# Block-sparse attention with a split-weight feed-forward layer: dense visits that take half of the keys for four heads

## The chip, the cores and the metric

One core of a Trainium2 chip runs the whole program. The metric is the device time of one execution in microseconds (us), the median of several runs; lower is better. Its engines are TensorE (PE, with its weight loads shown as PEld), VectorE (DVE), ScalarE (ACT), GpSimd (POOL) and SyncE (SP, which here only issues DMAs).

## The reference

Attention over 4 batches, 8 heads, 768 positions and a head size of 64, in float32, with a mask of 24 by 24 blocks of 32 positions; then a layer norm and a two-layer feed-forward part of widths 512, 2048, 512.

```python
mask = np.abs(blk_i - blk_j) <= window                       # window = 1
mask = mask | (blk_i == 0) | (blk_j == 0) | (blk_i == n_blocks - 1) | (blk_j == n_blocks - 1)
for qb in range(n_blocks):
    for kb in sampled_blocks[qb]:                            # 3 per row
        mask[qb*block:(qb+1)*block, kb*block:(kb+1)*block] = True
scores = np.where(mask, scale * (q @ k.T), -1e9)
attn = softmax(scores)                                       # row maximum subtracted
x = (attn @ v), heads side by side
xn = (x - mu) / np.sqrt(var + 1e-06) * g_ln
out = x + np.maximum(xn @ w_ch1, 0.0) @ w_ch2
```

A row of an inner block sees at most 8 blocks of keys (256 keys). Rows of block 0 and block 23 see all 768 keys.

## The kernel before, in words

The 768 positions of a batch are reordered into six tiles of 128 rows. Five of them hold four inner blocks each; the sixth (`t == 0`) holds blocks 1, 2, 0 and 23. Tiles run in the order 1, 2, 3, 0, 4, 5 for each of the four batches. The work on a tile is cut into visits, 15 per batch and 60 in all, and a job is the visits that share one load of keys and values:

- an N job (tiles 1 to 5) has two visits, each with four heads of all 128 rows against the 256 gathered keys of each row's block;
- tile 0 has an H job (one visit: blocks 1 and 2, all eight heads, 256 gathered keys) and a D job with four dense visits (blocks 0 and 23, 64 rows, all 768 keys, two heads each, so that 2 heads x 64 rows fill 128 partitions).

Called by their place in a batch, the D visits are the first to the fourth; the N visit after them belongs to tile 4. In a visit `scores` (line 195, its matmuls in `mm`, L203) multiplies queries and keys into one two-bank PSUM tile `ps` (1024 columns), `biggest` (L233) takes the row maximum on DVE, `softmax` (L242) writes the exponentials to `p` on ACT, `turn` (L249) transposes `p` by chunks of 128 columns on PE and copies them on ACT, and, one visit later, `attn_v` (L259) multiplies with the values into `pv` and `evict` (L291) divides by the row sum on DVE (the 65th column of the values is 1).

A matmul of scores contracts over 64 partitions and has 32 output partitions: the row half of the array is the parity `j` of the head, the column group is the 32-row piece `part`. An N visit gives the two row halves in turn (`j` = 0, 1, each to its own PSUM bank). A D visit has one parity:

```python
            j = vi.r % 2
            for lo, hi in ((0, 16), (16, 24)):
                for rr in range(2):
                    pr = 2 * vi.hf + rr
                    for gg in range(2):
                        mm(j, 2 * rr + gg, 32 * lo, 32 * (hi - lo), ...)
```

The order of the work is written out by a loop over steps. In step s come the scores and the maximum of visit s, then `attn_v` and `evict` of visit s-1, then `softmax` of s, and then pieces of the feed-forward part (`ffn`: up-projection L349 into `pu`, L359 on ACT and L360 on DVE make `hh` and `hl` of it; down-projection L373 into `pd`), shared out by a fixed cost per matmul. The pieces go around `turn` of s and around the loads of the next job, which are issued in the first visit of a job (`keys`, `values`). So the keys of a D job are issued in the H visit: `keys` sends two DMAs of 12 blocks each (L134, 768 KB each) with the values (L176, 1560 KB) between them on SP's queue. There are two buffers for keys (`ks`) and for values (`vs`): the tile-5 job loads into those of the D job, in the step of the N visit after the D visits. For an N job SP sends the neighbours' keys (L144) and values (L180, L188) and twelve gathered key blocks (L153), and POOL gathers sampled value blocks with four indirect DMAs (L192) into chunks 0, 2, 4, 6 of `vs`. Every engine runs its own stream in order; the waits between engines are set by the tile framework from what each instruction reads and writes. The weights are split into two float16 parts while the first visits run.

Of the kernel before, what the change touches and what calls it, by code (L numbers as in the profile page):

```python
# [25 lines left out]
def sparse_attention_moe(  # L26
# [169 lines left out]
    def scores(vi):  # L196
# [10 lines left out]
        if vi.kind == "N":  # L207
            for pp in range(2):
                pr = 2 * vi.hf + pp
                for gg in range(4):  # L210
                    for j in range(2):
                        mm(j, gg, 512 * j + 256 * pp, 256, q[:, pr, 32 * gg : 32 * gg + 32],
                           ks[:, gg, :, 32 * pr : 32 * pr + 32])
        elif vi.kind == "H":
            for pp in range(2):
                for rr in range(2):
                    pr = 2 * pp + rr
                    for gg in range(2):
# [13 lines left out]

    def biggest(vi):  # L233
        n, w = vi.shape
        st = vi.st = sm.tile([P, 8], F32, tag="st", name=f"st{vi.i}")
        nc.vector.tensor_reduce(out=st[:, 0:n],  # L236
                                in_=vi.ps[:, 0 : n * w].rearrange("p (h k) -> p h k", k=w),
                                axis=AX.X, op=ALU.max, negate=True)
        nc.vector.tensor_scalar(out=st[:, 4 : 4 + n], in0=st[:, 0:n], scalar1=0.125,
                                scalar2=None, op0=ALU.mult)  # L240

    def softmax(vi):  # L242
        n, w = vi.shape
        for h in range(n):
            hs = slice(h * w, (h + 1) * w)
            nc.scalar.activation(p_s[:, hs], vi.ps[:, hs], AF.Exp, bias=vi.st[:, 4 + h : 5 + h],  # L246
                                 scale=0.125)

    def turn(vi):  # L249
        c = vi.shape[0] * vi.shape[1] // P  # L250
# [8 lines left out]
    def attn_v(vi):  # L259
        pt, vs = pt_s[vi.i % 2], vi.job.vs  # L260
        pv = vi.pv = ps_v.tile([P, 512], F32, tag="pv", name=f"pv{vi.i}")
        nch = 6 if vi.kind == "D" else 2
        begun = set()

        def mm(row, col, ch, vv, e, c):
# [17 lines left out]
                                mm(2 * rr + gg, 2 * pp + j, (2 * j + pp) * 2 + c,  # L283
                                   2 * gg + c, h, c)
        else:
            for c in range(6):
                for rr in range(2):
                    for gg in range(2):
                        mm(2 * rr + gg, 0, c, c, 4 * vi.hf + 2 * rr + vi.r % 2, c)

    def evict(vi):  # L291
        n = 1 if vi.kind == "D" else 4
        u = vi.pv[:, 0 : n * 65].rearrange("p (h e) -> p h e", e=65)
        rs = sm.tile([P, n, 1], F32, tag="rs", name=f"rs{vi.i}")
        nc.vector.tensor_scalar(out=rs, in0=u[:, :, D : D + 1], scalar1=1e-9, scalar2=None,  # L295
                                op0=ALU.add)
# [5 lines left out]
            return  # L302
        for rr in range(2):
            rows = slice(64 * rr, 64 * rr + 64)
            if vi.kind == "D":
                h = 4 * vi.hf + 2 * rr + vi.r % 2
                nc.vector.tensor_scalar(out=x[64:128, h * D : (h + 1) * D], in0=u[rows, 0, 0:D],
                                        scalar1=rs[rows, 0, :], scalar2=None, op0=ALU.mult)
            else:
                for pp in range(2):  # L310
                    o = x[0:64, (4 * pp + 2 * rr) * D : (4 * pp + 2 * rr + 2) * D]
                    nc.vector.tensor_mul(o.rearrange("p (j d) -> p j d", d=D),
                                         u[rows, 2 * pp : 2 * pp + 2, 0:D],
                                         rs[rows, 2 * pp : 2 * pp + 2, :].to_broadcast([64, 2, D]))

    def norm_a(t):
        st = sm.tile([P, 10], F32, tag="ln", name=f"ln{t.n}")
# [125 lines left out]
    def add(t, kind, blocks, plan):  # L443
# [3 lines left out]
        jobs.append(job)  # L447
        for hf, r, heads in plan:
            vi = SimpleNamespace(i=len(visits), kind=kind, hf=hf, r=r, b=t.b, tile=t, job=job,
                                 heads=heads, shape=(1, 768) if kind == "D" else (4, 256))  # L450
            visits.append(vi)
            job.visits.append(vi)
            t.visits.append(vi)

    for t in tiles:
        t.visits = []
        if t.t:
            add(t, "N", list(range(4 * t.t - 1, 4 * t.t + 3)),
                [(f, f, list(range(4 * f, 4 * f + 4))) for f in range(2)])
        else:  # L460
            add(t, "H", [1, 2], [(0, 0, list(range(8)))])
            add(t, "D", [0, NB - 1], [(r // 2, r, [4 * (r // 2) + r % 2, 4 * (r // 2) + r % 2 + 2])
                                      for r in range(4)])
    NV = len(visits)
    NLAST = visits[-1].i

# [158 lines left out]
```

## Time and profile before

| what | value |
|---|---|
| median of 3 runs | 812.19 us (811.87 to 813.76) |
| the profiled execution | 817.5 us, span 815.7 us |
| PE busy | 717.9 us (88% of the span) |
| DVE, ACT, POOL busy | 314.2, 278.3, 210.8 us (39%, 34%, 26%) |
| DMA, mean over the span | 162 GB/s, 132.16 MB |
| mean granted TensorE clock | 0.955 |

The profiled execution took 5.3 us longer than the median. Times in rows are microseconds from the start of the span, durations are microseconds where not marked ns. A float32 matmul has two records in the trace, so the 16 matmuls of an N visit's scores are 32 records and the 8 of a D visit are 16. In a row of the timeline, what stands in square brackets is the idle time of the engine just before, and who ended it by the trace; "issue" means that the profile shows nothing that the engine waited for.

### The profile page before, as it was taken

To read this page: it belongs to the slowest core of one execution; us is meant where nothing else is said; L and a number is where in the kernel's file an instruction comes from. 1 tells how busy PE (TensorE), PEld (TensorE's weight loads), DVE (VectorE), ACT (ScalarE), POOL (GpSimd) and SP (SyncE) were. 2 spreads that over 40 slices of the span, in tenths; PEclk is the share of its full clock that TensorE was granted. 3 is DMA by queue.
4 is the path that set the end of the run, shared out by engine and by line. 5 is a ranking of instruction groups with operands and counts; after the bars stand their busy time and mean duration, and the time that the engine had idled before them with its cause. 6 is when DMAs were issued, how large, how long until landed. Compare 5 with 4: busy or idle time off the path is not lost.

```text
span 815.7 us, 21773 instructions
## 1 busy us (share of the span) xinstructions
PE 717.9 (88%) x9344; PEld 483.8 (59%) x9344; DVE 314.2 (39%) x618; ACT 278.3 (34%) x553; POOL 210.8 (26%) x236
## 2 busy tenths in 40 slices
PE   0545565999999999999999999989999999989997
PEld 0234432675685774765774856755866846756764
DVE  2577877334242341443341432333432332342211
ACT  0356454233343341342342431343432422333200
POOL 5276547121412103023230202023321020200000
PEclk9966786799999999999999999999999999999999
DMA  8997789138938439168947367168757194261000
GB/s 332 260 322 194 279 259 248 53 89 201 259 107 223 123 103 282 32 158 224 229 97 185 99 198 207 41 161 233 215 138 185 33 277 128 70 141 40 14 27 14
DMA packets 109792, 132.16 MB, mean 162 GB/s; under 512 B 34561, under 2 KB 80897, under 8 KB 108673
## 3 DMA queue, kind: packets, MB, share of 16 engines
q1 hardware_dynamic: 96848, 83.92, 40.0%
q0 software_dynamic: 12416, 46.51, 17.7%
q8 instruction: 74, 1.21, 0.6%
q10 hardware_dynamic: 432, 0.34, 0.1%
q14 instruction: 22, 0.17, 0.1%
HBM read 118.15 MB, written 6.29 MB: 153 GB/s over the span
## 4 chain that ended last, share of the span: by engine, by line
PE 55%; issue 20%; DMA 13%; POOL 5%; SPq 4%; DVE 2%; ACT 1%; POOLq 0%
PE pu L349 24%; PE pd L373 16%; PE ps L203 7%; DMA vs<-v 6%; PE pv L266 5%; PE pt L256 4%; DMA ks<-kT 4%; SPq L153 3%; DMA q<-qT 2%; POOL w2l L413 2%; POOL vs L192 1%; DVE ot L404 1%; POOL xl L327 1%; DMA samp<-sampled 1%; POOL ks L168 0%
## 5 line engine op out<-in xcount | busy, mean ns | idle before, releaser
L246 ACT ACTIVATE p<-ps,st 128x256 f32<-128x256 f32 (+1 forms) x192 | 83.3, 510 | 273.4 <-DVE rs L295 164.8
L349 PEld LDWEIGHTS <-w1h 128*128 128x128 f16 x1664 | 152.7, 99 | 18.6 <-issue 0.3
L373 PE MATMUL pd<-w2l,hh 128*128 128x512 f16 x384 | 147.5, 384 | 8.2 <-POOL w2l L413 4.5
L373 PE MATMUL pd<-w2h,hh 128*128 128x512 f16 x384 | 147.3, 384 | 3.1 <-ACT w2h L412 3.1
L373 PE MATMUL pd<-w2h,hl 128*128 128x512 f16 x384 | 147.5, 384 | 0.0
L360 DVE SCALAR_TENSOR_TENSOR hl<-pu,hh 128x512 f16<-128x512 f32 x96 | 66.4, 692 | 181.1 <-ACT hh L359 180.2
L373 PEld LDWEIGHTS <-hh 128*128 128x128 f16 x768 | 75.4, 99 | 94.5 <-issue 13.2
L203 PE MATMUL ps<-ks,q 64*32 64x256 f32 (+1 forms) x1664 | 83.5, 420 | 47.6 <-DMA ks<-kT 26.2
L349 PE MATMUL pu<-xth,w1l 128*128 128x256 f16 (+1 forms) x832 | 120.6, 266 | 0.0
L349 PE MATMUL pu<-xth,w1h 128*128 128x256 f16 (+1 forms) x832 | 120.6, 266 | 0.0
L349 PE MATMUL pu<-xtl,w1h 128*128 128x256 f16 (+1 forms) x832 | 120.5, 265 | 0.1
L236 DVE TENSOR_REDUCE st<-ps 128x4 f32<-128x1024 f32 (+1 forms) x60 | 69.1, 1151 | 122.6 <-PE ps L203 122.6
L192 POOL DMA_INDIRECT vs<-v,rows x88 | 87.9, 998 | 99.1 <-PE pv L266 60.5
L359 ACT ACTIVATE hh<-pu 128x512 f16<-128x512 f32 x96 | 57.4, 598 | 125.0 <-PE pu L349 110.9
L256 PE MATMUL pt<-id_sb,p 128*128 128x128 f32 x448 | 67.5, 293 | 28.4 <-ACT p L246 28.4
L203 PEld LDWEIGHTS ps<-ks,q 64*32 64x32 f32 x1664 | 34.8, 110 | 85.6 <-issue 75.0
L257 ACT COPY pt<-pt 128x512 f32<-128x512 f32 x120 | 62.1, 564 | 64.7 <-PE pt L256 56.9
L349 PEld LDWEIGHTS <-w1l 128*128 128x128 f16 x832 | 78.2, 99 | 8.5
L256 PEld LDWEIGHTS pt<-id_sb,p 128*128 128x128 f32 x448 | 54.9, 149 | 40.1 <-ACT p L246 33.4
L379 DVE SCALAR_TENSOR_TENSOR ot<-pd,x 128x512 f32<-128x512 f32 x24 | 16.6, 690 | 156.5 <-PE pd L373 156.5
L266 PEld LDWEIGHTS pv<-vs,pt 128*32 128x32 f32 x3584 | 56.5, 112 | 32.9 <-issue 24.1
L266 PE MATMUL pv<-vs,pt 128*32 128x65 f32 x3584 | 67.9, 225 | 5.1 <-issue 2.9
(75 smaller groups left out, 416.4 us busy)
## 6 DMA issues: line engine op xcount, KB each, us to landing
ks<-kT SPq DMA_DIRECT2D x28, 768.0 KB
ks<-kT SPq DMA_DIRECT2D x264, 64.0 KB
vs<-v SPq DMA_DIRECT2D x20, 780.0 KB
vs<-v SPq DMA_DIRECT2D x4, 1560.0 KB
q<-qT SPq DMA_DIRECT2D x24, 256.0 KB
out<-ot POOLq DMA_DIRECT2D x24, 256.0 KB
vs<-v SPq DMA_DIRECT2D x16, 260.0 KB
w2h<-w POOLq DMA_DIRECT2D x4, 1024.0 KB
```

The source lines that it names most:

```text
L153: nc.sync.dma_start(kv[:, gg, r, :], src[:, bass.ds(reg[NR * gg + r], 1), :] .rearrange("p o e -> p (o e)"))
L192: nc.gpsimd.indirect_dma_start(out=vs[:, 2 * gg, :], out_offset=None, in_=src, in_offset=bass.IndirectOffsetOnAxis(ap=rows[:, i : i + 1], ...
L203: nc.tensor.matmul(ps[32 * part : 32 * part + 32, col : col + n], lhs[64 * row : 64 * row + 64], rhs[64 * row : 64 * row + 64], start=True ...
L236: nc.vector.tensor_reduce(out=st[:, 0:n], in_=vi.ps[:, 0 : n * w].rearrange("p (h k) -> p h k", k=w), axis=AX.X, op=ALU.max, negate=True)
L246: nc.scalar.activation(p_s[:, hs], vi.ps[:, hs], AF.Exp, bias=vi.st[:, 4 + h : 5 + h], scale=0.125)
L256: nc.tensor.transpose(pt[:, k - lo, :], p_s[:, k * P : (k + 1) * P], id_sb)
L257: nc.scalar.copy(dst[:, lo:hi, :], pt[:, 0 : hi - lo, :])
L266: nc.tensor.matmul(pv[32 * row : 32 * row + 32, 65 * col : 65 * col + 65], pt[:, ch, 32 * row : 32 * row + 32], vs[:, vv, 65 * e : 65 * e ...
L349: nc.tensor.matmul(ph[:, j * n : (j + 1) * n], w[:, ct, fs], x[:, ct, 0:n], start=m == 0, stop=m == 3 * CT - 1, skip_group_check=True)
L359: nc.scalar.activation(dh, ph, AF.Relu)
L360: nc.vector.scalar_tensor_tensor(out=dl, in0=ph, scalar=0.0, in1=dh, op0=ALU.max, op1=ALU.subtract)
L373: nc.tensor.matmul(po, x[:, f, ts], w[:, f, :], start=m == 0, stop=m == 3 * FT - 1)
```

## The change

The four D visits of a tile stay four visits, with the same loads and the same place in the order. A visit now takes 384 keys (blocks 0 to 11 or 12 to 23, by `vi.r`) for four heads (two pairs, both parities), in place of 768 keys for two heads. The first and second visit make the two halves for heads 0 to 3, the third and fourth those for heads 4 to 7. Each half has its own row maximum. The second half of a pair works out the weights of the two halves (three small DVE operations and an exponential of 4 columns), and its `evict` scales both halves by them, adds them and divides. The first half's `evict` only copies `pv` out of PSUM.

```diff
@@ scores
-            j = vi.r % 2
-            for lo, hi in ((0, 16), (16, 24)):
-                for rr in range(2):
-                    pr = 2 * vi.hf + rr
-                    for gg in range(2):
-                        mm(j, 2 * rr + gg, 32 * lo, 32 * (hi - lo),
-                           q[:, pr, 64 + 32 * gg : 96 + 32 * gg],
-                           kx[:, lo:hi, 32 * pr : 32 * pr + 32])
+            half = slice(12 * vi.r, 12 * vi.r + 12)
+            for rr in range(2):
+                pr = 2 * vi.hf + rr
+                for gg in range(2):
+                    for j in range(2):
+                        mm(j, 2 * rr + gg, 512 * j, 384, q[:, pr, 64 + 32 * gg : 96 + 32 * gg],
+                           kx[:, half, 32 * pr : 32 * pr + 32])
@@ biggest
+        if vi.kind == "D" and vi.r:
+            a, c = vi.mate.st[:, 4:6], st[:, 4:6]
+            nc.vector.tensor_tensor(out=st[:, 6:8], in0=a, in1=c, op=ALU.min)
+            nc.vector.tensor_sub(st[:, 8:10], st[:, 6:8], a)
+            nc.vector.tensor_sub(st[:, 10:12], st[:, 6:8], c)
@@ softmax
         for h in range(n):
...
+        if vi.kind == "D" and vi.r:
+            nc.scalar.activation(vi.st[:, 12:16], vi.st[:, 8:12], AF.Exp)
@@ attn_v
-            for c in range(6):
-                for rr in range(2):
-                    for gg in range(2):
-                        mm(2 * rr + gg, 0, c, c, 4 * vi.hf + 2 * rr + vi.r % 2, c)
+            for j in range(2):
+                for c in range(3):
+                    for rr in range(2):
+                        for gg in range(2):
+                            mm(2 * rr + gg, j, 3 * j + c, 3 * vi.r + c, 4 * vi.hf + 2 * rr + j, c)
@@ evict
+        if vi.kind == "D":
+            half = sm.tile([P, 2, 65], F32, tag="half", name=f"half{vi.i}")
+            if not vi.r:
+                nc.vector.tensor_copy(half, u)
+                vi.half = half
+                return
+            wt = vi.st[:, 12:16].rearrange("p (r h) -> p r h", r=2).unsqueeze(3)
+            nc.vector.tensor_mul(half, u, wt[:, 1].to_broadcast([P, 2, 65]))
+            both = vi.mate.half
+            nc.vector.tensor_mul(both, both, wt[:, 0].to_broadcast([P, 2, 65]))
+            nc.vector.tensor_add(half, half, both)
+            u = half
@@ jobs
-                                 heads=heads, shape=(1, 768) if kind == "D" else (4, 256))
+                                 heads=heads, shape=(2, 384) if kind == "D" else (4, 256))
```

No instruction changes its place against those of other visits; the number of feed-forward matmuls per step is the same. Two places show what the streams look like. The first is PE's stream at the first D visit of batch 1 (`ps_3507` before, `ps_3521` after; `pd` is the down-projection ahead of it, `pv` the H visit's product with the values; the names in brackets are the semaphores waited for, and DMAHW6 and DMAHW0 are those of the first and the second key DMA). Before:

```order
L373 MATMUL pd_3429<-w2h,hl 128x512
L373 LDWEIGHTS hh
L373 MATMUL pd_3429<-w2l,hh 128x512
L203 MATMUL ps_3507<-ks_80,q_89 32x512 [waits DMAHW6_49,DMAHW0_49,DVE_49]
L203 MATMUL ps_3507<-ks_80,q_89 32x512 x3
L203 MATMUL ps_3507<-ks_80,q_89 32x256 x4
L266 MATMUL pv_3519<-vs_83,pt_87 32x65 [waits DMASW7_49,DVE_49,Activation_49]
```

And now:

```order
L390 MATMUL pd_3443<-w2h,hl 128x512
L390 LDWEIGHTS hh
L390 MATMUL pd_3443<-w2l,hh 128x512
L203 MATMUL ps_3521<-ks_80,q_89 32x384 [waits DMAHW6_49,DVE_49]
L203 MATMUL ps_3521<-ks_80,q_89 32x384 x7
L274 MATMUL pv_3533<-vs_83,pt_87 32x65 [waits DMASW7_49,DVE_49,Activation_49]
```

The first visit's scores no longer name the second key DMA; the second visit's do. The second place is DVE's stream in the N visit after the D visits (`st_4027` before, `st_4051` after, is that visit's maximum; then comes `evict` of the fourth D visit; `hl` is the feed-forward part). Before:

```order
L236 TENSOR_REDUCE st_4027<-ps_4010 128x4 [waits PE_49]
L239 TENSOR_SCALAR st_4027<-st_4027 128x4 [waits DVE_49]
L295 TENSOR_SCALAR rs_4055<-pv_4030 128x1 [waits PE_49]
L297 RECIPROCAL rs_4055<-rs_4055 128x1 [waits DVE_49]
L307 TENSOR_SCALAR x_94<-pv_4030,rs_4055 64x64 [waits DVE_49]
L307 TENSOR_SCALAR x_94<-pv_4030,rs_4055 64x64
L360 SCALAR_TENSOR_TENSOR hl<-pu_12_3988,hh 128x512 [waits Activation_49]
```

And now:

```order
L239 TENSOR_REDUCE st_4051<-ps_4034 128x4 [waits PE_49]
L240 TENSOR_SCALAR st_4051<-st_4051 128x4 [waits DVE_49]
L310 TENSOR_TENSOR half_4079<-pv_4054,st_3927 128x130 [waits PE_49]
L312 TENSOR_TENSOR half_3958<-half_3958,st_3927 128x130
L313 TENSOR_TENSOR half_4079<-half_4079,half_3958 128x130 [waits DVE_49]
L316 TENSOR_SCALAR rs_4083<-half_4079 128x2 [waits DVE_49]
L318 RECIPROCAL rs_4083<-rs_4083 128x2 [waits DVE_49]
L329 TENSOR_TENSOR x_94<-half_4079,rs_4083 64x128 [waits DVE_49]
L329 TENSOR_TENSOR x_94<-half_4079,rs_4083 64x128
L377 SCALAR_TENSOR_TENSOR hl<-pu_12_4012,hh 128x512 [waits Activation_49]
```

Three operations of 130 columns stand ahead of the four that were there, and `hl` behind them.

## Rows read from the trace of the kernel before

**Rows 1.** The page, part 1: busy us, share of the span, instructions.

```profile
PE 717.9 (88%) x9344; PEld 483.8 (59%) x9344; DVE 314.2 (39%) x618; ACT 278.3 (34%) x553; POOL 210.8 (26%) x236
```

**Rows 2.** Busy time by stretch: stretch, length, each engine's busy us, clock, DMA share, GB/s.

```profile
311.20:351.70 40.50, 40.50 (x509) 27.86 (x508) 12.92 (x33) 10.42 (x18) 6.99 (x10) 1.00 0.45 129
```

**Rows 3.** Timeline, PE: scores of the first D visit, batches 1, 2, 3.

```profile
311.10 1.49 PE L203 MATMUL ps<-ks,q 64*32 64x512 f32 x16 [1.29 <-DVE ot L379]
...
488.42 1.49 PE L203 MATMUL ps<-ks,q 64*32 64x512 f32 x16 [0.46 <-DMA ks<-kT]
...
666.47 1.50 PE L203 MATMUL ps<-ks,q 64*32 64x512 f32 x16 [1.20 <-DMA ks<-kT]
```

**Rows 4.** Timeline, PE: scores of a D visit, of the N visit behind, of batch 0's second.

```profile
333.70 1.49 PE L203 MATMUL ps<-ks,q 64*32 64x512 f32 x16
...
351.71 1.09 PE L203 MATMUL ps<-ks,q 64*32 64x256 f32 x32
...
145.34 2.79 PE L203 MATMUL ps<-ks,q 64*32 64x512 f32 x16
```

**Rows 5.** Timeline, SP's queue: the D job's loads in batch 1.

```profile
299.05 0.57 SPq L134 DMA_DIRECT2D ks<-kT  x1
299.81 0.38 SPq L176 DMA_DIRECT2D vs<-v  x1
300.24 0.53 SPq L134 DMA_DIRECT2D ks<-kT  x1
```

**Rows 6.** Timeline, third D visit of batch 1 on DVE, ACT and PEld.

```profile
335.26 0.96 DVE L236 TENSOR_REDUCE st<-ps 128x1 f32<-128x768 f32 x1 [0.90 <-PE ps L203]
...
336.52 0.90 ACT L246 ACTIVATE p<-ps,st 128x768 f32<-128x768 f32 x1 [2.89 <-DVE rs L295]
...
337.92 0.69 PEld L256 LDWEIGHTS pt<-id_sb,p 128*128 128x128 f32 x6
...
338.64 0.69 DVE L360 SCALAR_TENSOR_TENSOR hl<-pu,hh 128x512 f16<-128x512 f32 x1 [1.35 <-ACT hh L359]
```

**Rows 7.** Lines, by form, whole span: count, busy us, mean ns, idle before.

```profile
L246 ACT ACTIVATE p<-ps,st 128x256 f32<-128x256 f32 x176 | 68.9, 474 | 198.2 <-DVE rs L295 98.6 <-DVE st L239 73.2 <-PE pd L373 22.6
...
L312 DVE TENSOR_TENSOR x<-pv,rs 64x128 f32<-64x128 f32 x16 | 3.9, 283 | 0.2
```

**Rows 8.** Timeline, the N visit after the D visits, batch 1.

```profile
352.74 0.89 PE L266 MATMUL pv<-vs,pt 128*32 128x65 f32 x48
...
353.36 0.98 POOL L192 DMA_INDIRECT vs<-v,rows  x1 [7.90 <-PE pv L266]
...
356.90 0.34 SPq L180 DMA_DIRECT2D vs<-v  x1
356.90 0.16 DVE L295 TENSOR_SCALAR rs<-pv 128x1 f32<-128x1 f32 x1 [2.56 <-PE pu L349]
...
357.15 0.95 POOL L192 DMA_INDIRECT vs<-v,rows  x1 [0.30 <-issue]
...
359.06 0.38 PE L373 MATMUL pd<-w2l,hh 128*128 128x512 f16 x1 [0.96 <-issue]
```

**Rows 9.** Timeline, PE: the same stop in batches 0, 2 and 3.

```profile
182.56 0.38 PE L373 MATMUL pd<-w2l,hh 128*128 128x512 f16 x1 [0.97 <-issue]
...
536.35 0.38 PE L373 MATMUL pd<-w2l,hh 128*128 128x512 f16 x1 [0.91 <-issue]
...
714.42 0.38 PE L373 MATMUL pd<-w2l,hh 128*128 128x512 f16 x1 [0.73 <-issue]
```

**Rows 10.** Timeline, PE: scores of tile 5's first visit, batches 0 to 3.

```profile
196.45 1.43 PE L203 MATMUL ps<-ks,q 64*32 64x256 f32 x32 [1.19 <-issue]
...
372.90 1.52 PE L203 MATMUL ps<-ks,q 64*32 64x256 f32 x32 [1.14 <-DMA q<-qT]
...
551.10 1.52 PE L203 MATMUL ps<-ks,q 64*32 64x256 f32 x32 [2.04 <-DMA q<-qT]
...
728.56 1.52 PE L203 MATMUL ps<-ks,q 64*32 64x256 f32 x32 [1.87 <-issue]
```

More of the change, by code (lines that the diff above doesn't have):

```diff
@@ L223, in scores, with seen @@
         else:
-            j = vi.r % 2
-            for lo, hi in ((0, 16), (16, 24)):
-                for rr in range(2):
-                    pr = 2 * vi.hf + rr
-                    for gg in range(2):
-                        mm(j, 2 * rr + gg, 32 * lo, 32 * (hi - lo),
-                           q[:, pr, 64 + 32 * gg : 96 + 32 * gg],
-                           kx[:, lo:hi, 32 * pr : 32 * pr + 32])
-    def biggest(vi):
[L234 to L238, printed above, removed]
+            half = slice(12 * vi.r, 12 * vi.r + 12)
[5 more added lines that the diff above has]
+                           kx[:, half, 32 * pr : 32 * pr + 32])
+    def seen(vi):
+        n, w = vi.shape
+        return vi.ps.rearrange("p (h k) -> p h k", h=n)[:, :, 0:w]
+    def biggest(vi):
+        n = vi.shape[0]
+        st = vi.st = sm.tile([P, 16], F32, tag="st", name=f"st{vi.i}")
+        nc.vector.tensor_reduce(out=st[:, 0:n], in_=seen(vi), axis=AX.X, op=ALU.max, negate=True)
         nc.vector.tensor_scalar(out=st[:, 4 : 4 + n], in0=st[:, 0:n], scalar1=0.125,
                                 scalar2=None, op0=ALU.mult)
+        if vi.kind == "D" and vi.r:
[3 more added lines that the diff above has]
+            nc.vector.tensor_sub(st[:, 10:12], st[:, 6:8], c)
     def softmax(vi):
@@ L244, in softmax @@
         for h in range(n):
-            hs = slice(h * w, (h + 1) * w)
-            nc.scalar.activation(p_s[:, hs], vi.ps[:, hs], AF.Exp, bias=vi.st[:, 4 + h : 5 + h],
-                                 scale=0.125)
+            nc.scalar.activation(p_s[:, h * w : (h + 1) * w], seen(vi)[:, h, :], AF.Exp,
+                                 bias=vi.st[:, 4 + h : 5 + h], scale=0.125)
+        if vi.kind == "D" and vi.r:
+            nc.scalar.activation(vi.st[:, 12:16], vi.st[:, 8:12], AF.Exp)
     def turn(vi):
@@ L261, in attn_v @@
         pv = vi.pv = ps_v.tile([P, 512], F32, tag="pv", name=f"pv{vi.i}")
-        nch = 6 if vi.kind == "D" else 2
+        nch = 3 if vi.kind == "D" else 2
         begun = set()
@@ L285, in attn_v @@
         else:
-            for c in range(6):
-                for rr in range(2):
-                    for gg in range(2):
-                        mm(2 * rr + gg, 0, c, c, 4 * vi.hf + 2 * rr + vi.r % 2, c)
+            for j in range(2):
[3 more added lines that the diff above has]
+                            mm(2 * rr + gg, j, 3 * j + c, 3 * vi.r + c, 4 * vi.hf + 2 * rr + j, c)
     def evict(vi):
-        n = 1 if vi.kind == "D" else 4
+        n = 2 if vi.kind == "D" else 4
         u = vi.pv[:, 0 : n * 65].rearrange("p (h e) -> p h e", e=65)
+        if vi.kind == "D":
[10 more added lines that the diff above has]
+            u = half
         rs = sm.tile([P, n, 1], F32, tag="rs", name=f"rs{vi.i}")
@@ L304, in evict @@
             rows = slice(64 * rr, 64 * rr + 64)
[L305 to L314, printed above, removed]
+            for pp in range(n // 2):
+                h = 4 * (vi.hf if vi.kind == "D" else pp) + 2 * rr
+                o = x[64:128, h * D : (h + 2) * D] if vi.kind == "D" else x[0:64, h * D : (h + 2) * D]
+                nc.vector.tensor_mul(o.rearrange("p (j d) -> p j d", d=D),
+                                     u[rows, 2 * pp : 2 * pp + 2, 0:D],
+                                     rs[rows, 2 * pp : 2 * pp + 2, :].to_broadcast([64, 2, D]))
     def norm_a(t):
@@ L461, in sparse_attention_moe @@
             add(t, "H", [1, 2], [(0, 0, list(range(8)))])
-            add(t, "D", [0, NB - 1], [(r // 2, r, [4 * (r // 2) + r % 2, 4 * (r // 2) + r % 2 + 2])
+            add(t, "D", [0, NB - 1], [(r // 2, r % 2, list(range(4 * (r // 2), 4 * (r // 2) + 4)))
                                       for r in range(4)])
+            for r in (1, 3):
+                jobs[-1].visits[r].mate = jobs[-1].visits[r - 1]
     NV = len(visits)
```

## The prediction

> **What bounds the kernel now.** I read the page's busy shares first, then the busy time by stretch, then every idle time of PE in the timeline. The shares say PE, at 88% of the span [rows 1]. By stretch it is stricter: from the first D visit of batch 1 to the N visit behind the fourth, PE is busy 40.50 of 40.50 us at the full granted clock (1.00, the level of 2.4 GHz), DVE 12.92 and ACT 10.42 [rows 2]. A D visit there lasts 9.0 us (two of them from 333.70 to 351.71 [rows 4]), most of it feed-forward matmuls, so what PE saves inside a D visit shortens the kernel, and DVE and ACT have room. In all batches behind the start PE stands still in few places, and three kinds bear on this change: ahead of the first D visit's scores [rows 3], in the N visit behind the D visits [rows 8, 9], and ahead of tile 5's first scores [rows 10].
>
> **Scores, the main term.** A D visit's scores take 1.49 us, an N visit's 1.09 us [rows 4]. Before, a D visit uses one row half: four column groups side by side, 512 and then 256 columns, each with two records. In units of one 256-column record per group that is (2 + 1) x 2 = 6 units in a row. An N visit uses both row halves: 16 matmuls of 256 columns on eight places, 2 x 2 = 4 units. Two units less cost 0.40 us less, so a unit is 0.20 us. Now a D visit has eight matmuls of 384 columns on eight places, 1.5 x 2 = 3 units: 1.09 - 0.20 = 0.89 us, and 0.60 us saved. Twelve visits of batches 1 to 3 save 7.2 us, all on PE's path. In batch 0 the third and fourth save another 1.2 us; the second ran at the lower granted clock and took 2.79 us [rows 4], so the same share of it is 1.1 us; the first I count at nothing, since PE waits for the weight split behind it. Sum **9.5 us**. The bounds: nothing if the row halves take turns (a rival below), and 0.745 us a visit, half of 1.49, if no fixed part is left, which is 2.4 us more.
>
> **First half of the keys.** PE waits 1.29, 0.46 and 1.20 us ahead of the first D visit [rows 3]. The trace blames a key DMA in two of the three; in batch 1 it names a DVE result, and I take it for the same wait. SP sends the first key half at 299.05, the values at 299.81, the second half at 300.24 [rows 5], and the scores, which need both halves, start at 311.10 [rows 3]: 768 + 1560 + 768 KB in some 12 us. The new first visit needs the first half alone. If the DMAs land in order, it is there after a quarter of the bytes, some 3 us; if all three share the bandwidth evenly from the start, 3 x 768 of 3096 KB have moved when it lands, after 9 us, at about 308. PE comes free at 309.81 (311.10 less its wait), later than either. So the whole wait goes: **2.95 us**; the lower bound is 0. Next late would be the second half, but the second visit starts 9 us later.
>
> **Products with the values, transposes.** 24 matmuls of 65 columns and 6 transposes a visit, as before: 0.
>
> **Exponentials.** One of 768 columns took 0.90 us [rows 6], one of 256 takes 0.474 [rows 7]: 0.83 ns a column, so one of 384 takes 0.58 and two 1.16, or 0.26 more. In the third D visit of batch 1 the exponential ended at 337.42 and PE loaded weights for the transposes at 337.92 [rows 6]: 0.50 us of slack, 0.24 left. The row maximum reads as many columns (0.96). The transposes of the first head also need only the first exponential. So 0. If each of the two cost 0.90, the second would be 0.40 us late. The exponential of the weights, at most 0.47, comes behind both and holds up only copies that PE needs a visit later.
> What this row says is weighed against a rule. The Trainium skill, "TensorEngine Tiling (Array Packing)", section Performance Considerations (PSUM Bottleneck), warns that packing speeds up TensorE but not the reading of PSUM, which may become the bound. By it the 9.5 us would be partly given back as PE waits at the transposes; by the row's slack nothing is.
>
> **Combining the halves.** The first and third visits' results now need one copy in place of four operations. The second and fourth visits' need three operations more, at 0.28 us each by the 128-column row [rows 7]: 0.85 us, and three tiny ones at the maximum. In the third D visit (which evicts the second's result) DVE then idles 1.35 us ahead of `hl` [rows 6], which covers it. In the N visit `hl` follows at once, but it is for the last columns of the up-projection, and the down-projection takes three matmuls for each of 16 groups of columns in turn, and this is group 12 at the earliest, 36 matmuls on. So 0; the upper bound is 4 x 0.85 = 3.4 us if PE waits there.
>
> **The late signal.** In the N visit behind the D visits, the product with the values ends at 353.63, yet SP's values DMA and DVE's division start only at 356.90 [rows 8]. That is the end of POOL's third gather (the fourth starts at 357.15 after 0.30 us [rows 8]). PE then stands 0.96 us and goes on at 359.06, which is 0.96 us after the end of the fourth gather (357.15 + 0.95). The same stop is there in every batch, 0.97, 0.91 and 0.73 us [rows 9]. I do not know the mechanism, only that it goes with the four gathers that start while the product still runs. The change touches their start: the gathers write chunks 0, 2, 4, 6 of the D job's values, and chunks 0 and 2 belong to blocks 0 to 11, which are last read by the third D visit. So two gathers may go a visit earlier and two are left in the burst, which then ends 2.5 us sooner. I take it that PE's four stops go, **3.57 us**; the lower bound is 0.
>
> **Sum.** 9.5 + 2.95 + 3.57 = 16.0 us. The profiled execution's own time of 817.5 would become 801.5; the median stands 5.3 us below it, so the forecast is 812.19 - 16.0 = **796.2 us**.
>
> **The rivals.** A change within 0.3% (2.4 us) is what a measurement of this kernel cannot tell from none.
> - *The signal comes in time.* If SP is also released at once, the loads for tile 5 start 3.3 us earlier, and the waits of 1.19, 1.14, 2.04 and 1.87 us ahead of tile 5's scores [rows 10] go as well: 6.24 us more, **790.0 us**. For it: the loads are in SP's order behind that DMA, and all four waits are shorter than 3.3 us. Against it: two gathers remain. Chance 0.25.
> - *The stops stay.* The gathers cost PE as much in two pieces, or stops seen in a profiled execution, 5.3 us slower, are less in the timed ones: 812.19 - 12.45 = **799.7 us**. Chance 0.27.
> - *PSUM reading becomes the bound.* With 0.40 us late in 16 visits and the stops kept: 799.7 + 6.4 = **806.1 us**. The slack of 0.24 speaks against it. Chance 0.08.
> - *The row halves take turns.* Then a visit's scores keep six units, 1.49 us, and only the keys' wait goes: **809.2 us**, hardly a change. N visits with the same alternation of halves and banks speak against it. Chance 0.04.
> - *Slower: the packing breaks.* If only two of the eight matmuls ran at once, the scores would need 12 units, 1.49 + 6 x 0.20 = 2.69 us, or 1.20 us more in 16 visits: 812.19 + 19.2 - 2.95 = **828.4 us**. It decides from 1.67 us a visit on, where 16 x 0.18 eats the 2.95. Nothing in N visits speaks for it. Chance 0.03.
>
> **How the numbers follow.** The forecast has the remaining 0.33. Faster by over 0.3%: the forecast and the first three rivals, 0.93; the same 0.04; slower 0.03. The range takes in 790.0 and 799.7 with 1.5 us below and the 3.4 us bound of the combination above, 788.5 to 803.5: 0.85 of the chance.
>
> **What would show it.** Right: D visits' scores near 0.89 us; no idle ahead of the first D visit; transposes that do not wait for `p`; three operations near 0.28 us on DVE; two gathers in the fourth D visit; no stop of PE behind the D visits. Wrong: scores above 1.1 us, PE idle with ACT or DVE as releaser in D visits, or the waits of [rows 10] grown by what was saved.

## The result and the profile after

The changed kernel takes 792.12 us in the median (789.92 to 794.32), the kernel before 812.21 us beside it: a ratio of 0.9754, 95% interval 0.9727 to 0.978. That is 20.1 us less, faster by more than the 16.0 us forecast; inside its range. It is within about 2 us of the rival "the signal comes in time" (790.0 us), and that rival's mechanism is what the trace shows.

The two profiled executions differ by more than the medians, 817.5 to 789.92 us: that of before stood 5.3 us above its median, that of after 2.2 us below. Sums of steps below are of these two traces.

The page of the changed kernel, part 1, answers to [rows 1]:

```profile
PE 703.4 (89%) x9344; PEld 478.3 (61%) x9344; DVE 319.1 (40%) x642; ACT 282.3 (36%) x577; POOL 210.7 (27%) x236
```

PE is busy 14.5 us less with as many instructions; DVE has 24 instructions more and ACT 24 more, 4.9 and 4.0 us. The stretch from the first D visit of batch 1 to the N visit behind the fourth answers to [rows 2]:

```profile
303.29:341.44 38.15, 38.15 (x511) 27.01 (x510) 14.34 (x37) 11.23 (x24) 9.31 (x12) 1.00 0.61 156
```

It is 38.15 us in place of 40.50 [rows 2] (a stretch that leaves out the first 0.10 us of the scores), and the 1.29 us of wait ahead of it [rows 3] is gone too. PE is still busy all of it. The scores on PE's timeline, the first, third and fourth D visit of batch 1, the N visit behind the fourth, and batch 0's second D visit, answer to [rows 3, 4]:

```profile
303.29 0.88 PE L203 MATMUL ps<-ks,q 64*32 64x384 f32 x16
...
324.66 0.88 PE L203 MATMUL ps<-ks,q 64*32 64x384 f32 x16
333.05 0.88 PE L203 MATMUL ps<-ks,q 64*32 64x384 f32 x16
...
341.44 1.09 PE L203 MATMUL ps<-ks,q 64*32 64x256 f32 x32
...
145.20 1.53 PE L203 MATMUL ps<-ks,q 64*32 64x384 f32 x16
```

0.88 us in place of 1.49, an N visit unchanged, and no idle time in brackets ahead of the first D visit. The D visit itself, from one's scores to the next's, is 8.39 us (324.66 to 333.05) in place of 9.01. The third D visit of batch 1 on DVE, ACT and PEld answers to [rows 6]:

```profile
325.64 0.96 DVE L239 TENSOR_REDUCE st<-ps 128x2 f32<-128x768 f32 x1 [0.32 <-PE ps L203]
...
326.92 1.05 ACT L252 ACTIVATE p<-ps,st 128x384 f32<-128x384 f32 x2 [2.32 <-DVE st L240]
...
328.26 0.69 PEld L264 LDWEIGHTS pt<-id_sb,p 128*128 128x128 f32 x6
```

The two exponentials end at 327.97, 0.29 us ahead of the weight loads for the transposes. The combination of two halves, lines by form (count, busy, mean ns, idle before), answers to [rows 7]:

```profile
L310 DVE TENSOR_TENSOR half<-pv,st 128x130 f32<-128x130 f32 x8 | 2.3, 286 | 0.0
L312 DVE TENSOR_TENSOR half<-half,st 128x130 f32<-128x130 f32 x8 | 2.3, 286 | 0.0
L313 DVE TENSOR_TENSOR half<-half,half 128x130 f32<-128x130 f32 x8 | 2.4, 296 | 0.3
```

And the N visit behind the D visits in batch 1, with the gathers of the fourth D visit ahead of it (PE, POOL, SP, DVE), answers to [rows 8]:

```profile
335.38 0.99 POOL L192 DMA_INDIRECT vs<-v,rows  x1 [0.15 <-issue]
336.67 0.95 POOL L192 DMA_INDIRECT vs<-v,rows  x1 [0.30 <-issue]
...
342.46 0.89 PE L274 MATMUL pv<-vs,pt 128*32 128x65 f32 x48
...
343.41 0.34 SPq L180 DMA_DIRECT2D vs<-v  x1
...
343.54 0.94 POOL L192 DMA_INDIRECT vs<-v,rows  x1 [5.92 <-PE pv L274]
344.79 0.95 POOL L192 DMA_INDIRECT vs<-v,rows  x1 [0.30 <-issue]
...
343.97 0.29 DVE L310 TENSOR_TENSOR half<-pv,st 128x130 f32<-128x130 f32 x1
```

Two gathers have gone a visit earlier. SP sends the values 0.06 us after the product's end (342.46 + 0.89 = 343.35), where it came 3.27 us late [rows 8], and DVE starts as soon as its maximum is done. PE has no stop there in any batch [rows 8, 9], and no wait ahead of tile 5's scores [rows 10]. Behind batch 0 two waits are left:

```profile
PE ps L203 <- DMA q<-qT: 8.8, 2, 7.5
...
PE ps L203 <- DVE ot L396: 1.3, 1, 1.3
```

(the view of waits: us in total, times, longest.) 1.3 us each, ahead of tile 1's scores of batches 2 and 3; the 7.5 us lie in batch 0.

Where the time came from, by the steps from one visit's scores to the next, before less after, all batches: D visits 7.4 us in batches 1 to 3 and 3.4 in batch 0 (1.60 of it the second, whose first 6.1 us before and 4.2 us after ran at a granted clock of 0.50, the level of 1.2 GHz, so that not all of it is the scores'); H visits 3.15; the N visit behind the D visits 1.23, 1.24, 1.22, 1.23, so 4.9; the next visit, at whose end the wait for tile 5 stood, 1.26, 1.21, 2.06, 1.93, so 6.5; tile 5's first visit 1.1, since its scores took 1.43 to 1.52 us behind that wait [rows 10] and take 1.09 to 1.43 now. That is 26.4 of 27.7 us.

Another 2.2 us (1.07, 1.00 and 0.11) lie in tile 5's second visits of batches 0 to 2, and the other steps together lose 0.9. In that visit of batch 1 the kernel before (POOL, PE, DVE) has

```profile
383.77 0.94 POOL L192 DMA_INDIRECT vs<-v,rows  x1 [0.30 <-issue]
...
384.53 0.62 PE L266 MATMUL pv<-vs,pt 128*32 128x65 f32 x11
385.64 1.01 PE L266 MATMUL pv<-vs,pt 128*32 128x65 f32 x53 [0.50 <-issue]
...
385.83 1.23 DVE L236 TENSOR_REDUCE st<-ps 128x4 f32<-128x1024 f32 x1 [6.50 <-PE ps L203]
```

and the changed one

```profile
370.71 0.95 POOL L192 DMA_INDIRECT vs<-v,rows  x1 [0.30 <-issue]
...
371.56 1.23 DVE L239 TENSOR_REDUCE st<-ps 128x4 f32<-128x1024 f32 x1 [5.30 <-PE ps L203]
```

The scores end at 384.60 before and at 371.45 after. DVE takes their maximum 1.23 us behind that end before and 0.11 after, and only before does PE stop inside the product (0.69, 0.50 and 0.50 us in batches 0 to 2). The gather beside it is the last of four for the next batch's tile 1; the first of them starts 4.5 us after the product that they wait for. The change does not touch this place, and the runs below divide there by chip and not by kernel, so these 2.2 us are not put down to the change.

### The profile page after: what moved, and what is told of

It reads as the page before. It is cut to its first block, busy times and chain, and to the rows that moved or that the text cites. A ratio compares the mean times of both kernels' runs of the same rounds, so it can differ in the third digit from the quotient of the medians.

```text
span 788.0 us, 21825 instructions
## 1 busy us (share of the span) xinstructions
PE 703.4 (89%) x9344; PEld 478.3 (61%) x9344; DVE 319.1 (40%) x642; ACT 282.3 (36%) x577; POOL 210.7 (27%) x236
## 3 DMA queue, kind: packets, MB, share of 16 engines
q8 instruction: 74, 1.21, 0.7%
## 4 chain that ended last, share of the span: by engine, by line
PE 67%; issue 16%; DMA 6%; POOL 5%; DVE 4%; SPq 1%; ACT 1%; POOLq 0%; ACTq 0%
PE pu L366 27%; PE pd L390 23%; PE ps L203 6%; PE pv L274 6%; PE pt L264 5%; DMA ks<-kT 2%; DMA vs<-v 2%; POOL w2l L430 2%; DMA q<-qT 1%; POOL vs L192 1%; DVE ot L421 1%; POOL xl L344 1%; SPq L153 1%; DMA samp<-sampled 0%; DVE ot L419 0%
## 5 line engine op out<-in xcount | busy, mean ns | idle before, releaser
L252 ACT ACTIVATE p<-ps,st 128x256 f32<-128x256 f32 (+1 forms) x208 | 86.0, 491 | 257.1 <-DVE rs L316 156.6
L203 PE MATMUL ps<-ks,q 64*32 64x256 f32 (+1 forms) x1664 | 71.8, 421 | 39.3 <-DMA ks<-kT 24.3
L264 PE MATMUL pt<-id_sb,p 128*128 128x128 f32 x448 | 65.9, 289 | 30.0 <-ACT p L252 30.0
L344 POOL TENSOR_TENSOR xl<-xn,xh 128x512 f16<-128x512 f32 x24 | 27.7, 1156 | 165.0 <-ACT xh L343 164.8
L203 PEld LDWEIGHTS ps<-ks,q 64*32 64x32 f32 x1664 | 29.7, 109 | 66.6 <-issue 57.7
```

Source lines behind the costliest of these rows:

```text
L203: nc.tensor.matmul(ps[32 * part : 32 * part + 32, col : col + n], lhs[64 * row : 64 * row + 64], rhs[64 * row : 64 * row + 64], start=True ...
L252: nc.scalar.activation(p_s[:, h * w : (h + 1) * w], seen(vi)[:, h, :], AF.Exp, bias=vi.st[:, 4 + h : 5 + h], scale=0.125)
L264: nc.tensor.transpose(pt[:, k - lo, :], p_s[:, k * P : (k + 1) * P], id_sb)
L344: nc.gpsimd.tensor_sub(xl, xn, xh)
```

## The experiments

Theory: the three terms are right, and the last has a cause: a gather that POOL starts while the product with the values still runs holds back that product's last signal, which costs PE the stop and, by SP's late loads, the wait for tile 5. Rivals are named with each run. In the program as built, POOL's first gather in the N visit is let go after the 4th of the product's 24 matmuls in the kernel before (chunk 0 is read first), and after the 20th in the changed one (the first of the two gathers left writes chunk 4, which the second head's fifth group of four reads last). The kernel before was timed beside each run on the same chip; its medians were 809.9 to 819.9 us, so ratios are compared, and traces behind batch 0.

b_again, b_chunk0_last, a_upper_first and a_keys_late ran on chip 5 (the kernel before 816.2 us), a_again, a_early_gather, a_scores_alone and a_q_first on chip 7 (810.8), a_long_product, a_combine_x3 and a_j_outer on chip 10 (819.87), a_long_safe on chip 11 (809.93); that of the first pair is not known. Ratios do not take all of this out: a_again, the changed kernel itself, has 0.9726 on chip 7, while a_j_outer and a_combine_x3, which are nearly the changed kernel, have 0.9644 and 0.9648 on chip 10. And the delay in tile 5's second visit, DVE's maximum 1.2 to 1.4 us late and PE stopped in the product, is in the first three batches of all seven traces from chips 5 and 10, whatever the kernel, and in none of the five from chips 7 and 11. So a comparison across chips has a rival, the chip.

**b_again.** The kernel before once more, nothing edited.

> The kernel before, unchanged, profiled once more. Theory (the late signal belongs to the kernel: four gathers that start while the fourth D visit's product with the values still runs): PE stands again 0.7 to 1.0 us in the N visit behind the D visits of each batch, SP's values DMA there starts about 3.3 us after the product ends, and tile 5's first scores wait again 1.1 to 2.0 us. Rival (they belong to that one execution, which took 817.5 us where the median is 812.2): the stops and waits are gone or much smaller in this profile.

816.61 us. The N visit in batch 1 (PE, POOL, SP):

```profile
354.56 0.89 PE L266 MATMUL pv<-vs,pt 128*32 128x65 f32 x48
...
355.18 0.98 POOL L192 DMA_INDIRECT vs<-v,rows  x1 [7.90 <-PE pv L266]
...
357.73 0.95 POOL L192 DMA_INDIRECT vs<-v,rows  x1 [0.30 <-issue]
...
358.71 0.34 SPq L180 DMA_DIRECT2D vs<-v  x1
...
360.86 0.38 PE L373 MATMUL pd<-w2l,hh 128*128 128x512 f16 x1 [0.99 <-issue]
```

The same picture: SP at the end of the third gather, PE's stop of 0.99 us. The stops belong to the kernel. The waits for tile 5 are there too, but 0.79, 1.28, 1.55 and 0.43 us, 4.05 together in place of 6.24 [rows 10]: they vary between executions, one reason why the profiled pair differs by more than the medians.

**b_chunk0_last.** One part of the change's effect alone, in the kernel before: the first gather has to wait for the whole product.

```diff
-            for c in range(6):
+            for c in reversed(range(6)):
```

(the flag that ends the accumulation moves to chunk 0 with it.)

> The kernel before with only the order of the six chunks turned round in the D visits' product with the values: chunk 0 is read last, so POOL's first gather can start only after the whole product, and all four still stand in the N visit. Theory (the signal comes late because the gathers start while the product still runs): SP's values DMA and DVE's division follow the product at once, the waits ahead of tile 5 go, and the time falls by 3 to 10 us, to 802 to 809 us. Rival (it is the four gathers in a row beside the up-projection that hold PE's signals back, whenever they start): the late signal and the stop stay, 812 us.

807.13 us, 0.9861 of before (0.9807 to 0.9915). The same rows:

```profile
351.99 0.34 SPq L180 DMA_DIRECT2D vs<-v  x1
...
351.15 0.89 PE L266 MATMUL pv<-vs,pt 128*32 128x65 f32 x48
...
352.34 0.98 POOL L192 DMA_INDIRECT vs<-v,rows  x1 [8.47 <-PE pv L266]
...
352.66 0.15 DVE L296 TENSOR_SCALAR rs<-pv 128x1 f32<-128x1 f32 x1
```

SP comes 0.84 us after the product's start; the four gathers follow; DVE's division starts at 352.66, right behind its maximum, where it had waited 2.56 us [rows 8]. PE has no stop there in any batch, and three of the four waits for tile 5 are gone (batch 0 keeps 0.56 us). By the steps from the N visit behind the D visits to tile 5's first, the trace is 10.3 us shorter than that of b_again on the same chip. The order of six loop turns is worth 1.4%, some 11 us of 812 (7 to 16 by the interval), where the forecast had 3.57 and the rival 9.81.

**a_upper_first.** The changed kernel with the key halves swapped, so that chunks 0 and 2 are free only behind the fourth product and all four gathers stand behind it again. The first is let go after the 16th matmul.

```diff
-            half = slice(12 * vi.r, 12 * vi.r + 12)
+            half = slice(12 - 12 * vi.r, 24 - 12 * vi.r)
...
-                            mm(2 * rr + gg, j, 3 * j + c, 3 * vi.r + c, 4 * vi.hf + 2 * rr + j, c)
+                            mm(2 * rr + gg, j, 3 * j + c, 3 - 3 * vi.r + c, 4 * vi.hf + 2 * rr + j, c)
```

(the loads of the halves are swapped too.)

> The changed kernel with the halves exchanged: blocks 12 to 23 first, their keys also loaded first. Scores and the keys' wait stay as in the change; but chunks 0 and 2 of the values are now last read by the fourth D visit, so all four gathers stand behind its product again. Theory (the gathers' place is worth the rest of the gain): PE's stop of 0.7 to 1.0 us and the late values DMA come back in the N visit, with the waits ahead of tile 5, so the time is 5 to 10 us above the change (about 797 to 802 us). Rival (the gathers' place does nothing; the gain is scores and keys): same as the change, 792 us, and two gathers more in the N visit without a stop.

793.04 us, 0.9694 (0.964 to 0.9748). The stops did not come back: product at 344.27, SP at 345.11, the first of four gathers at 345.24, DVE's combination at 345.79, right behind its maximum. So the number of gathers behind the product is not what counts; the expectation's theory, as it was put, fell.

**a_early_gather and a_again.** To let the first gather go earlier, after the 8th matmul, the product of a_upper_first runs over chunks outermost (`for c in range(3): for j in range(2):`). The changed kernel ran beside it.

> The changed kernel once more, as the base for the three others of this call. Expected: 0.975 of the kernel before (0.973 to 0.978); D visits' scores 0.88 us, no stop of PE in the N visit behind the D visits, waits of 1.3 us ahead of tile 1's scores of batches 2 and 3.

> The changed kernel with the key halves swapped (first visit of a pair takes the upper half), and the product with the values running over chunks outermost, so that chunk 0 is read by the first 8 of the 24 matmuls and POOL's first gather is freed while 16 are still to run. Scores, key wait, number of matmuls and gathers as in the run with the halves swapped alone. Theory (the product's last signal is late whenever a gather is let go while the product still runs): SP's values DMA and DVE come some 3 us after the product's end, at the end of the third gather; PE stops 0.7 to 1.0 us in the N visit behind the D visits and waits ahead of tile 5's scores again: 4 to 10 us more than the changed kernel. Rival (the signal was late for something else in the kernel before, such as its four-operation eviction or its longer visits): within 2.4 us of the changed kernel.

a_again: 787.88 us, 0.9726 (0.9699 to 0.9753). a_early_gather: 791.83 us, 0.9783 (0.9751 to 0.9815).

```profile
346.62 0.34 SPq L180 DMA_DIRECT2D vs<-v  x1
...
346.64 0.98 POOL L192 DMA_INDIRECT vs<-v,rows  x1 [7.99 <-PE pv L274]
...
345.89 0.89 PE L274 MATMUL pv<-vs,pt 128*32 128x65 f32 x48
```

The time is near the lower end of what the theory gave, but the trace does not have its mechanism: DVE, which needs the last signal, starts on the product at 347.41, right behind its maximum, and PE doesn't stop. The first gather started 0.14 us before the product's end (346.78 by the row); in the kernel before it was 0.27 us (353.63 less 353.36 [rows 8]). So this run hardly made the condition it was built for: a gather that starts at the very end of the product delays nothing here. Whether that is a margin of the theory or chip 7, of which no trace of the kernel before was kept, stays open. By trace it is 4.8 us behind a_again, 3.2 of it in batch 0 (where two traces of the changed kernel differ by 0.9 us as well) and 1.6 ahead of tile 1's scores; why, stays open.

**a_long_product and a_long_safe.** The condition made certain: the fourth visit's product gets 16 matmuls more, into columns that nobody reads, so that it still runs when the first gather starts; and the control, the same 40 matmuls with the gathers' chunks read last.

```diff
+            for c in (0, 2):
+                chunk(c, 0)
+            if vi is vi.job.visits[-1]:
+                chunk(1, 2)
+                chunk(1, 4)
+            chunk(1, 0)
```

(`chunk(c, col)` issues the eight matmuls of one chunk; the control has `chunk(1, 0)` first, and chunks 2 and 0 behind the added ones.)

> The early-gather kernel with a longer product in the fourth D visit: chunk 0, chunk 2, then 16 added matmuls on chunk 1 into columns that nobody reads, then chunk 1. Theirs is added work: 16 of the 24 in 0.89 us, some 0.5 us in each of four batches, 2 us in all. The first gather is let go after 8 of 40 matmuls, and starts some 0.75 us after the product's start, with about 0.6 us of the product still to run (in the early-gather run it started at the very moment of the last signal). Theory (a gather that starts before the product's last signal holds that signal up to a later gather's end): SP's values DMA comes 1 to 4 us after the product's end, at the end of a gather; PE stops again in the N visit behind the D visits, and the time is 5 to 11 us above the early-gather run. Rival (three gathers waiting on separate counts, or something else in the kernel before, is what delays it): SP within 0.2 us of the product's end, time 2 us above the early-gather run.

> The long-product kernel with the same 40 matmuls in another order: chunk 1, the 16 added ones, chunk 2, and chunk 0, which the first gather waits for, last. Theory (it is the gather let go while the product still runs, not the added matmuls, that cost the 15 us): only the added work is left, 0.5 us in each of four batches: 2 us above the early-gather run, 0.975 to 0.981 of the kernel before; SP's values DMA within 0.2 us of the product's end. Rival (the longer product costs it by itself): 0.985, as the long-product run.

a_long_product: 807.43 us, 0.9849 (0.9813 to 0.9885). a_long_safe: 789.25 us, 0.9781 (0.9704 to 0.9858). First the long product:

```profile
348.96 1.65 PE L274 MATMUL pv<-vs,pt 128*32 128x65 f32 x72
351.02 0.32 PE L274 MATMUL pv<-vs,pt 128*32 128x65 f32 x4 [0.41 <-issue]
351.75 0.33 PE L274 MATMUL pv<-vs,pt 128*32 128x65 f32 x4 [0.41 <-issue]
...
355.36 0.60 PE L374 MATMUL pu<-xtl,w1h 128*128 128x256 f16 x4 [0.71 <-issue]
...
349.70 0.98 POOL L192 DMA_INDIRECT vs<-v,rows  x1 [7.99 <-PE pv L274]
...
355.54 0.34 SPq L180 DMA_DIRECT2D vs<-v  x1
```

then the control:

```profile
342.74 1.35 PE L274 MATMUL pv<-vs,pt 128*32 128x65 f32 x80
...
343.69 0.34 SPq L180 DMA_DIRECT2D vs<-v  x1
...
344.39 0.98 POOL L192 DMA_INDIRECT vs<-v,rows  x1 [8.90 <-PE pv L274]
```

With the gather 0.74 us into a product that takes 1.35 us in the control, SP is released 3.5 us after the product's last matmul (351.75 + 0.33), PE goes through the rest of the product in pieces and stops again and again, and the N visit takes 14.45 us. With the same matmuls in a safe order it takes 10.55 us; in a_early_gather, without the added ones, 10.09. So the added work costs 0.46 us a visit, and the late product 3.9 in this batch, 3.2 to 4.6 in the four. (In the control SP waits for chunk 1 alone, whose last read lies ahead of the product's end; DVE starts at 344.25, right behind its maximum.)

That it is the order alone, this pair does not show: the two ran on different chips, their ratios are 0.0068 apart with intervals that overlap, and chip 11 is one of those on which tile 5's second visit has no delay. What chip 10 shows by itself is that SP comes 3.41 to 3.46 us late in the four N visits of the long product, where the gather starts inside the product, and 0.06 us after the end in all those of a_combine_x3 and a_j_outer, where it starts behind it; these two take 17 to 18 us less.

**a_scores_alone.** The early-gather kernel with the key halves loaded in the old order: meant to leave the scores alone.

> The run with the early gather, and the key halves loaded in the old order, so that the first D visit needs the half that is sent second. Of the change only the scores on both row halves are left. Theory: late signal and key wait are back, and 0.61 us is saved in each of 12 D visits and 1 to 2 us in batch 0: 8 to 9.5 us less than the kernel before (0.988 to 0.990). Rival (what the scores save is given back at the later stops and waits, which start from a fixed transfer): 3 to 6 us less (0.992 to 0.996).

795.45 us, 0.9808 (0.9781 to 0.9835), below both ranges expected. Since the early gather does not bring the late signal back, this is scores and prompt signal together, and it is to be read against b_chunk0_last, which ran on another chip. From batch 1's first scores to the last visit's the two traces take 508.60 and 504.75 us: 3.9 less, not the 7.4 that twelve D visits save (12.98 and 8.39 in them, as in the changed kernel). 1.5 of it is the key wait, which came out longer in this execution (1.09, 0.23, 1.57 against 1.08, 0.27, none). The other 2 us are given back at scores that wait for q, tile 1's above all:

```profile
384.22 1.43 PE L203 MATMUL ps<-ks,q 64*32 64x256 f32 x32 [1.69 <-DMA q<-qT]
```

PE arrives sooner and meets a transfer that does not. Against a_early_gather the key wait's term shows: 3.6 us between the medians, 0.25% by the ratios, whose intervals overlap.

**a_keys_late.** The changed kernel with the second key half sent first (`for lo in (12, 0):`).

> The changed kernel with only the order of the two key DMAs of a D job exchanged, so that the first D visit needs the one that is issued last. Theory (the wait ahead of the first D visit was the last key DMA, 2.95 us in three batches): PE waits there again 0.5 to 1.4 us in batches 1 to 3, and the time is about 3 us above the change (795 us). Rival (the wait had another cause, such as the DVE result that the trace named in batch 1): no wait, same as the change, 792 us.

793.2 us, 0.9681 (0.9625 to 0.9738): not told from the changed kernel by time. By trace the wait is back, in the three batches:

```profile
305.16 0.88 PE L203 MATMUL ps<-ks,q 64*32 64x384 f32 x16 [0.75 <-DVE ot L396]
...
477.48 0.88 PE L203 MATMUL ps<-ks,q 64*32 64x384 f32 x16 [0.98 <-DMA ks<-kT]
...
648.27 0.88 PE L203 MATMUL ps<-ks,q 64*32 64x384 f32 x16 [0.80 <-DVE ot L396]
```

2.53 us, where the changed kernel has none. It also shows that the releaser "DVE ot" in [rows 3] stood for the key DMA: only the order of the loads was edited. By time the wait does not show on this chip: a_upper_first, which does not have it, took 793.04 us. By the steps of the two traces its H visits are 2.7 us shorter, and 1.0 of that is left at the last visit.

**a_combine_x3.** The three operations of L310 to L313 done three times over, the added six into a tile that nobody reads.

> The changed kernel with the three operations that combine two halves done three times over on DVE (the six added ones write a tile that nobody reads), 6 x 0.28 = 1.7 us more in each of 8 visits. Theory (the combination is covered, since the columns that DVE makes next are used 36 matmuls later): within 2.4 us of the changed kernel. Rival (PE waits there, so that the combination costs what it takes): 8 x 1.7 = 13 us more, and by the same price the change itself pays 8 x 0.85 = 6.8 us for its three.

790.23 us, 0.9648 (0.9618 to 0.9677); a_j_outer, run beside it, is the nearest measure of the changed kernel there, 0.9644. In the N visit of batch 1 `x` is then made at 349.70, and the step is 10.08 us, as without. The combination is covered even at three times its length.

**a_j_outer.** The eight score matmuls with the row half as the outermost loop (`for j in range(2): for rr in range(2): for gg in range(2):`).

> The changed kernel with the eight score matmuls of a D visit in another order: the four column groups of the first row half, then the four of the second, in place of taking turns. Theory (all eight places work side by side, whatever the order): 0.88 us as before, no change in time. Rival (only neighbours on different row halves run together): up to 1.49 us a visit, up to 9 us more.

789.75 us, 0.9644 (0.9602 to 0.9687), and 0.88 us a D visit (324.64 and 333.03). The row halves work side by side whichever is issued first.

**a_q_first.** The changed kernel with the next tile's q sent first in a tile's first visit, ahead of the twelve key transfers on SP, since the waits that are left are for q.

```diff
-    for t in tiles[1:]:
-        at(tiles[t.n - 1].visits[0].i, load_q, t.n)
...
+            if vi is vi.tile.visits[0] and vi.tile.n + 1 < len(tiles):
+                pre = [(load_q, (vi.tile.n + 1,))] + pre
```

> The changed kernel with the next tile's q sent first in a tile's first visit, ahead of the twelve key transfers of 64 KB each on SP that now stand before it. Theory: the two waits of 1.34 and 1.35 us that PE has left behind batch 0 (ahead of tile 1's scores) are q's, so 2.7 us less than the changed kernel; in batch 0 the wait of 7.5 us passes to the keys and gives nothing. Rival (the keys land as late as q): the waits stay, named after the keys, and the time is within 1 us of the changed kernel.

785.4 us (784.86 to 786.93), 0.9693 (0.9667 to 0.9719), beside a_again's 787.88 (787.19 to 789.07): 2.5 us less, ranges that do not meet, and faster than both kernels. Its trace has no idle time of PE behind 146 us. In that pair of traces the waits that went are shorter (0.48, 0.45, 0.51) than in the first profile, and the spans are only 0.4 us apart (785.3 and 784.9): some 1.8 us gained around tile 1's scores, the rest lost in batch 0. Where the medians' 2.5 us come from is shown by them in part alone.

## Why the prediction was right, and where it was short

**Scores, 9.5 us.** Right in its unit: 0.88 us against 0.89 worked out from an N visit's 1.09, and 0.61 us a visit. With batch 0 the steps gave 7.4 + 3.4 = 10.8 us. What the step had not seen is that some of it is given back, above all ahead of tile 1's scores, where PE comes to wait for q: some 2 us in a_scores_alone, as far as its comparison across chips tells. The changed kernel waits 1.34 and 1.35 us there, the kernel before 1.21 and 0.35. Its rivals fell: the halves do not take turns, and the packing holds in either order (a_j_outer).

**First half of the keys, 2.95 us.** 3.15 in the steps, 2.53 back in a_keys_late, 3.6 between the medians of a_scores_alone and a_early_gather. Right, with its reason, by the traces; by time it is not clear of the noise.

**Exponentials and combination, 0.** Right. The slack was put at 0.24 us and is 0.29; two exponentials of 384 take 0.58 each, as worked out. The combination's cover holds for three times its length. By the Trainium skill's page "TensorEngine Tiling (Array Packing)", section Performance Considerations (PSUM Bottleneck), reading PSUM could have become the bound; this trace does not bear it out, PE never waits at the transposes of a D visit behind batch 0.

**The late signal, 3.57 us.** This is the step that failed, by its size: the stops were worth 4.9 us in the steps, and the waits for tile 5 [rows 10], kept in the forecast, went as well, 7.6 us with the scores behind them; b_chunk0_last puts the whole at some 11 us. The forecast left them in because "two gathers remain". It counted gathers, "four gathers that start while the product still runs"; by [rows 8] only the first does (353.36, the product's end 353.63, the second gather 354.65). What counts at this place is whether that first one is let go before the product's last signal, and that stood in the order of the loops: after the 4th of 24 matmuls before, after the 20th now. Shown on chip 5 by b_again and b_chunk0_last (order alone takes the delay away) and by a_upper_first (four gathers, no delay). That a gather let go early brings the delay into the changed kernel is shown on chip 10 by a_long_product; that its added matmuls have no part in it is shown only across chips, by a_long_safe. What holds the signal back is not shown.

**The sum.** 16.0 forecast; 20.1 measured. The traces' 27.7 contain 5.3 us by which the profiled execution of before stood above its median, part of it in waits for tile 5 that were longer there than in b_again, and 2.2 us by which that of after stood below. That the sum came as near as it did is in part luck: the signal's term was 7 to 8 us too small, while some of the scores' saving is given back, and the gain itself differs by chip (0.9754 in the first pair, 0.9726 on chip 7, about 0.965 for the nearest kernels on chip 10). The upper end of the range, 799.7 + 3.4, is 803.1 and not 803.5; nothing hangs on it.

## What to carry to other kernels

When POOL issues indirect DMAs behind a PE product that reads the same buffer, let the first of them wait for the product's last matmul: read the chunk that is overwritten first last (here 1.4%, in six loop turns). Packing row halves pays by the unit that a neighbour in the same trace shows, but count what PE then meets sooner: the transfers that were just in time become the next waits, and one reordered DMA may take them away. When a wait disappears with a cause that is not understood, look in the program for which instruction releases whom, and price everything that stands behind the released one.

## What the runs showed of the hardware that was not expected

An indirect gather on POOL (0.95 to 0.98 us each) can hold up signals from PE, which it has no part in. SP and DVE act on the product's last matmul 3.27 us late in [rows 8] and 3.26 in b_again (358.71 less 355.45) when the first of four gathers starts 0.27 us before the product's end, and 3.5 us late when it starts 0.74 us into a longer product (a_long_product). With 0.14 us left (a_early_gather, on another chip), or when the gathers start behind it, there is no delay: SP comes 0.06 us after the end in the changed kernel. During such gathers PE's own matmuls can come in groups with 0.41 us between them (a_long_product), and PE stops 0.99 us as late as behind the last gather (b_again, 360.86 against 358.98 + 0.95). Whether the signals queue, or PE's instructions do, no run here tells.

A gather beside PE's work is not enough for it. In tile 5's second visit the same kind of delay, DVE 1.2 to 1.4 us late and PE stopped for 0.49 us and more, stands in all traces from chips 5 and 10 and in none from chips 7 and 11, with the gather at the same place to 0.01 us: a_j_outer's starts 0.34 us after the scores' start and DVE is 1.34 us late, a_long_safe's 0.35 and 0.11. What differs between the chips, no run here tells, nor whether the kernel before has its late signal on chips 7 and 11.

The order of loops that made this hardly shows in busy time: in the N visit of batch 1 PE is busy 10.33 us in b_again and 10.09 in b_chunk0_last, the other engines differ by 0.1 us or less. It shows as idle time without a releaser ("issue") and as work that starts later than its input's end.
